# Two SSM convolution layers and two GEGLU layers on one core: another opening, and filter transforms moved from the opening into the layers

## The chip, the cores and the metric

The kernel runs on one core of a Trainium2 chip. The metric is the device time of one execution in microseconds. The engines are TensorE (PE, with its weight loads PEld), VectorE (DVE), ScalarE (ACT), GpSimd (POOL) and SyncE (SP); SP, ACT and POOL also issue DMA transfers, each in the order of its own queue. An instruction runs when its engine has come to it and what it waits for is done; the order on each engine is fixed when the program is built.

## The reference

Two kinds of layer alternate, A, B, A, B, over x of 2048 tokens by 576 channels; B's feed-forward width is 4608. All inputs are bf16.

```python
def _A_ref(q, k, v, shift_k, ssm_k, ssm_D):
    k_shift = sum over t in range(4) of k_pad[:, t:t + S, :] * shift_k[:, 3 - t]
    kv = k_shift * v
    y = causal convolution of kv with ssm_k along the tokens (by rfft2/irfft2 of length 2 * S)
    y = y + kv * ssm_D
    return q * y
def _B_ref(x, w_gate, w_up, w_down):
    return (_gelu(x @ w_gate) * (x @ w_up)) @ w_down

x = A_q
x = x + _A_ref(_layernorm(x), A_k, A_v, A_shift_k, A_ssm_k, A_ssm_D)
x = x + _B_ref(_layernorm(x), B_w_gate, B_w_up, B_w_down)
x = x + _A_ref(_layernorm(x), A_k, A_v, A_shift_k, A_ssm_k, A_ssm_D)
x = x + _B_ref(_layernorm(x), B_w_gate, B_w_up, B_w_down)
```

The convolution's result y does not depend on x: both A layers use the same y, computed once.

## The kernel before

**Convolution.** Tokens are cut into 4 blocks of 512. A block is transformed by matmuls with tables of cosines and sines (512 odd frequencies; kt is a tile of 128 frequencies of four, s is the cosine or the sine part). The spectrum of the product of k-block a and filter block b is added to output block a + b. `kv_ops` (L152 to L179) makes a block of kv on DVE: per pair of token rows four tap products (L162), three adds (L167) and a product with v (L172). `fwd_eo` (L201) transforms a block of kv: for kt 0 and 1 it sums even and odd token rows apart in PSUM, ACT copies them out, and two DVE operations (`cross`, L213) make kt and kt + 2 of them, so that four matmuls serve where eight would. `prod` (L217) multiplies spectra on DVE, `accumulate` (L231) sums products in PSUM by an identity matmul, `both`, `shifted` and `inverse` lead back to y.

**The opening** (`begin`, L475 to L691) is written out by hand. It makes a table G for the filter (angles on DVE, a mask, sines on ACT, four rounds, L534 to L541) and tables F1, F2 for kv. All four filter blocks are transformed in it (`h_tile`, `fwd_h` L181: eight matmuls for each kt and s, 16 tiles of 2 x 8) and stored in DRAM (Hd); block 1 also stays in SBUF (H1). Filter block 0 comes by a plain load and PE transposes (L551), blocks 1 to 3 by transposing DMAs on SP (L494). k block 0 is loaded by ACT's queue after two small loads, v block 0 by POOL's. Then come the kv of block 0, its transform (`fwd_full`, L190, with a negated copy of two token rows, L590), products (L224 to L228), pairs (L625), the inverse, the gate of layer A for the first 512 tokens (L792, L797), their normalising (L1003) and transposes into xnT (L1015). Between these stand the filter tiles of blocks 1 to 3 and the first 8 of the 16 kv operations of block 1.

**The layers.** The work of B is cut into 8 units (layer, block of 512 tokens) and each unit into 3 phases of 12 gate/up groups (18 matmuls of 512 columns, L1096) and the down projection (96 matmuls, L1112). Passes are [0], [1, 2], [3, 4], [5, 6], [7]: in a pass the phases are the outer loop, so pass 0 is unit 0 alone, and unit 1, tokens 512 to 1023 of the first B layer, is the first that needs y of block 1. Its xnT is written by transposing DMAs on SP (`spread`, L924).

**The planner.** `Pace` keeps an estimated clock for PE, DVE and ACT while the program is built. `fill` (L979) is called after each gate/up group and within the down projection. It issues due weight loads, loads of the convolution in the order of the list L (`run_loads`), tasks of DVE from two lists (`conv.run_v`: V with U ahead; `run_vq`: gates and normalising) as long as they end before a limit, and up to three pieces of PE work of the convolution (`run_p`, list Pq, in order). `conv.step(m)` enters block m in these lists. One PSUM buffer ("cps") is the convolution's, three ("pr") are the layers'. `load_k` and `load_v` have one SBUF buffer each (tags "k" and "v" of the pool c_kv).

## Time and profile before

| | |
|---|---|
| median of 3 runs | 964.27 us (962.89 to 965.34) |
| profiled execution, span | 963.7 us |
| first gate/up matmul (L1096) | 68.15 us |
| first gate/up matmul of unit 1 | 192.74 us |
| gate/up, L1096 | 5184 matmuls, 566.2 us |
| down, L1112 | 2304 matmuls, 296.9 us |
| filter transforms, L186 | 256 matmuls, 27.6 + 10.1 us, all before 68.3 us |
| transforms of kv in the layers, L207 | 96 matmuls, 15.7 us |
| sums of products, L234 | 144 matmuls, 24.7 us |
| PE busy, 0 to 10 / 10 to 20 / 20 to 30 / 50 to 60 us | 10.0 / 8.79 / 8.31 / 6.84 |
| DVE busy, 30 to 40 / 50 to 60 / 70 to 80 / 100 to 110 us | 9.69 / 4.62 / 7.82 / 8.97 |

Busy time of a line is the union of its instructions' spans. The spans of neighbouring matmuls overlap in the trace (two sums of L234 have 0.42 us together), so what a matmul costs in a stream is read from the period, one start to the next. A name like cps<-v,F is the output and the inputs by the program's names.

### The profile page before, as it was taken

Reading aid. Unit: us, or ns where it says so; the run is one execution under the profiler, and the core shown is the slowest. Engines: PE = TensorE matmul, PEld = TensorE weight load, DVE = VectorE, ACT = ScalarE, POOL = GpSimd, SP = SyncE. Lnnn points to the kernel's source line nnn. Section 1 sums busy time; section 2 is a strip of 40 time slices with the busy share of each in tenths; the row PEclk is TensorE's granted clock in tenths of the full one; section 3 lists DMA queues with packets and bytes.
Section 4 is the critical chain, followed back from the end, with each engine's and each line's share of the span. In section 5 each row is a group of like instructions: output and inputs, shape, how many; then the busy total and the mean of one; then the engine's idle time right before and its main releaser. Section 6 shows DMA issues by size and latency. Waiting matters only on the chain.

```text
span 963.7 us, 19315 instructions
## 1 busy us (share of the span) xinstructions
PE 948.0 (98%) x8256; PEld 546.6 (57%) x8256; DVE 538.8 (56%) x975; ACT 304.5 (32%) x557; POOL 139.7 (14%) x303
## 2 busy tenths in 40 slices
PE   6989999999999999999999999999999999999998
PEld 4764655646556566465565565565466466456455
DVE  7967887988785476888323333654323325522332
ACT  7866223541222523413212412342211213311211
POOL 2453210432101111412000100230000002100000
PEclk9999999999999999999999999999999999999999
DMA  6979994693942641495270270484450540396630
GB/s 166 312 192 287 300 199 126 112 224 134 264 148 75 130 131 49 100 240 129 51 170 3 57 166 7 90 147 105 89 134 1 100 123 2 77 253 148 155 71 26
DMA packets 129066, 127.48 MB, mean 132 GB/s; under 512 B 45587, under 2 KB 121684, under 8 KB 128980
## 3 DMA queue, kind: packets, MB, share of 16 engines
q1 hardware_dynamic: 119904, 90.85, 43.5%
q0 software_dynamic: 8944, 34.49, 11.0%
q8 instruction: 64, 1.05, 0.5%
q10 hardware_dynamic: 132, 0.91, 0.3%
q14 instruction: 22, 0.18, 0.1%
HBM read 105.58 MB, written 10.62 MB: 121 GB/s over the span
## 4 chain that ended last, share of the span: by engine, by line
PE 95%; DVE 3%; DMA 1%; ACT 1%; POOL 0%; issue 0%; SPq 0%; DVEq 0%
PE gu L1096 58%; PE dn L1112 30%; PE cps L234 2%; PE cps L207 1%; PE cps L260 1%; PE ps L186 1%; DMA hn<-in_A_ssm_k_dram 1%; PE cps L186 0%; DVE yb L228 0%; DVE prod L227 0%; DVE yb L625 0%; DVE stats L777 0%; DVE kvt L162 0%; DVE prod L224 0%; PE xps L1015 0%
## 5 line engine op out<-in xcount | busy, mean ns | idle before, releaser
L1096 PE MATMUL gu<-xnT,wgu 64*128 64x512 bf16 x5184 | 566.2, 376 | 0.0
L1096 PEld LDWEIGHTS <-wgu 64*128 64x128 bf16 x5184 | 249.1, 94 | 307.1 <-issue 9.0
L1101 DVE TENSOR_TENSOR hT<-ga,gu 128x512 bf16<-128x512 f32 x288 | 197.7, 687 | 265.2 <-ACT ga L1100 263.7
L1100 ACT ACTIVATE ga<-gu 128x512 f32<-128x512 f32 x288 | 172.0, 597 | 540.9 <-PE gu L1096 539.0
L1112 PE MATMUL dn<-wd,hT 128*128 128x288 bf16 x2304 | 296.9, 286 | 0.5 <-DVE ob L1121 0.5
L1112 PEld LDWEIGHTS <-hT 128*128 128x128 bf16 x2304 | 223.6, 98 | 66.2 <-issue 10.5
L1146 DVE TENSOR_TENSOR x_c<-x_c,dn 128x576 f32<-128x576 f32 x64 | 48.2, 753 | 92.5 <-PE dn L1112 92.1
L825 POOL TENSOR_SCALAR nm<-s 128x1 f32<-128x1 f32 x60 | 19.9, 332 | 369.9 <-DVE x_c L1141 170.6
L833 ACT ACTIVATE junk<-x_c,nm 128x576 bf16<-128x576 f32 x48 | 36.9, 769 | 27.4 <-POOL nm L825 27.4
L841 POOL TENSOR_TENSOR rstd<-ve,neghalf_t 128x1 f32<-128x1 f32 x60 | 38.3, 638 | 5.0
L228 DVE TENSOR_TENSOR sum<-prod 128x576 bf16<-128x576 bf16 x72 | 33.0, 458 | 3.1
L186 PEld LDWEIGHTS <-G 128*128 128x128 bf16 x256 | 26.1, 103 | 10.2 <-DVE h L553 1.3
L186 PE MATMUL ps<-h,G 128*128 128x288 bf16 x192 | 27.6, 300 | 1.8 <-DVE h L553 1.2
L318 POOL DMA_DIRECT2D kr<-Kd x24 | 13.2, 548 | 107.4 <-DVE prod L227 107.4
L1132 DVE TENSOR_TENSOR ob<-x_c,dn 128x576 bf16<-128x576 f32 x15 | 11.3, 755 | 29.0 <-PE dn L1112 19.9
L326 POOL DMA_DIRECT2D hr<-Hd x32 | 17.7, 553 | 52.8 <-DVE prod L227 52.7
L840 POOL TENSOR_SCALAR ve<-ss 128x1 f32<-128x1 f32 x60 | 17.7, 294 | 51.2 <-ACT junk L833 51.1
L234 PE MATMUL cps<-sum,ident 128*128 128x288 bf16 x144 | 24.7, 286 | 0.0
L162 DVE TENSOR_TENSOR kvt<-k,skc 128x1152 bf16<-128x1152 bf16 x32 | 23.8, 754 | 0.5
L215 DVE TENSOR_TENSOR kc<-eo 128x288 bf16<-128x288 f32 x48 | 19.4, 453 | 2.5 <-ACT eo L210 2.5
L210 ACT COPY eo<-cps 128x576 f32<-128x576 f32 x24 | 15.3, 637 | 16.4 <-PE cps L207 13.6
L268 POOL DMA_DIRECT2D out_dram<-ob x12 | 6.7, 555 | 88.0 <-DVE ob L1132 88.0
(114 smaller groups left out, 471.9 us busy)
## 6 DMA issues: line engine op xcount, KB each, us to landing
wgu<-in_B_w_gate_dram SPq DMA_DIRECT2D x45, 576.0 KB, 5.6
wd<-in_B_w_down_dram SPq DMA_DIRECT2D x30, 864.0 KB, 7.2
wgu<-in_B_w_up_dram SPq DMA_DIRECT2D x45, 512.0 KB, 7.5
hr<-Hd POOLq DMA_DIRECT2D x32, 288.0 KB, 6.6
kr<-Kd POOLq DMA_DIRECT2D x24, 288.0 KB, 5.2
Hd<-h POOLq DMA_DIRECT2D x12, 288.0 KB, 3.8
Kd<-kc POOLq DMA_DIRECT2D x12, 288.0 KB, 8.9
k<-in_A_k_dram POOLq DMA_DIRECT2D x3, 1008.0 KB, 10.4
```

Of the source, the lines that this page charges most:

```text
L162: nc.vector.tensor_tensor(out=st[dst][:], in0=self.kt_[b][:, s0:s0 + 2, :], in1=self.skc[:, j, :].unsqueeze(1).to_broadcast([P, 2, D]), op ...
L186: nc.tensor.matmul(ps[:, h, 0:HW], lhsT=G[:, i, s * NFQ + kt * P: s * NFQ + (kt + 1) * P], rhs=src[:, i, h * HW:(h + 1) * HW], start=(i == ...
L228: nc.vector.tensor_tensor(out=dst, in0=pr[:, 0, :], in1=pr[:, 1, :], op=ALU.subtract if part == 0 else ALU.add)
L234: nc.tensor.matmul(ps[:, h, 0:HW], lhsT=self.ident[:], rhs=pr[:, h * HW:(h + 1) * HW], start=first, stop=last)
L825: nc.gpsimd.tensor_scalar(out=v["nm"][:], in0=v["s"][:], scalar1=-1.0 / D, scalar2=None, op0=ALU.mult)
L833: nc.scalar.activation(out=junk[:], in_=get_x(), func=ACT.Square, bias=v["nm"][:, 0:1], accum_out=v["ss"][:])
L841: nc.gpsimd.tensor_tensor(out=v["rstd"][:], in0=ve[:], in1=neghalf_t[:, 0:1], op=ALU.pow)
L1096: nc.tensor.matmul(pair[:, s, :], lhsT=w[r0:r0 + HK, k, gi * P:(gi + 1) * P], rhs=xnT[r0:r0 + HK, b, :], start=(k == 0), stop=(k == NKC - 1))
L1100: nc.scalar.activation(out=ga[:], in_=pair[:, 0, :], func=ACT.Gelu_apprx_tanh)
L1101: nc.vector.tensor_tensor(out=hT[:, fi, :], in0=ga[:], in1=pair[:, 1, :], op=ALU.mult)
L1112: nc.tensor.matmul(acc[:, h, 0:HW], lhsT=hT[:, fi, j * P:(j + 1) * P], rhs=wd[2 * wb + fi // WT][:, fi % WT, h * HW:(h + 1) * HW], start=( ...
L1146: nc.vector.tensor_tensor(out=xh, in0=xh, in1=acc[:, :, 0:HW], op=ALU.add)
```

## The change

The function `begin` is gone. The opening is now written as tasks with an engine, a cost, dependences, PSUM banks and a priority; a class `Plan` puts them in order by a list schedule when the program is built, and then they are issued in that order. What the tasks do differs too:

- One table T of 128 frequencies (`tang`, `tmask`, `tsin`) and one table V for the way back serve everything. The other three tiles of frequencies are T with the planes exchanged or negated (`turned`, `fw`, `lhs`); DVE makes the negated planes (`tnegs`, `vnegs`). The filter is read in the token order of kv, so G, F1 and F2 fall away.
- The taps of k block 0 are multiplied on DVE, and the four products of a token row are summed in PSUM by identity matmuls; v multiplies that sum from PSUM.
- The skip weight ssm_D is added to the filter before its transposes, on POOL, from a load of single columns (`dcol`).
- Only filter block 0 is transformed in the opening, and sent to DRAM. Block 1 is loaded and transposed there by PE (`turned_h(1)`) into the buffer of tag "v". Blocks 2 and 3 are read by a transposing DMA on SP and written to DRAM again in natural order (`natural`, hs). `conv.step(m)` then transforms filter block m by `fwd_h`, which uses `fwd_eo`, so that 4 matmuls serve where 8 did, as 8 pieces in Pq ahead of the pieces of kv; Hd is stored after it, and hr is loaded from Hd for every pair (block 1 is no longer resident). v of block m is loaded after those pieces, into the same buffer.
- All 16 kv operations of block 1 are in the layers.
- The inverse of block 0 stays in PSUM and the gate reads it there; ACT copies y out afterwards.
- The first three gate/up groups are cut in two: their halves for token rows 0 and 2 (256 columns) stand in the opening, the halves for rows 1 and 3 in the layers' loop. These three and the convolution's bank take the four PSUM banks.
- The queues: k block 0 is the first load on ACT's; sk1, the small parts of k, the filter, v, x_b and filter block 1 go by SP's, followed by wgu 0, wgu 1, filter block 2, wgu 2 (after block 1's transposes), wd 0, wd 1, filter block 3, wd 2.

The core of the diff:

```diff
+    def order(self, cold):
...
+            task.rank = task.cost + task.lat + max([u.rank for u in task.users_of], default=0.0)
...
+            for eng, found in seen.items():
+                first = min(at for at, _ in found)
+                at, task = max(((at, k) for at, k in found if at <= first + 0.25), key=lambda f: (f[1].rank + f[1].prio, -f[0]))
...
+    def turned(self, s, r):
+
+        return s ^ (r & 1), r in ((2, 3) if s == 0 else (1, 2))
...
+        def lh():
+            self.load_ht(m, nc.gpsimd)
+            at["h"] = t.pe + 9.0
+        if loaded:
+            at["k"] = at["h"] = 0.0
+        else:
             self.L.append((lambda: self.kv_at.get(m - 1, NEVER), lk))
-            self.L.append((lambda: self.fwd_at.get(m - 1, NEVER), lv))
-        else:
-            at["k"] = at["v"] = 0.0
+            self.L.append((lambda: self.fwd_at.get(m - 1, NEVER), lh))
+        self.L.append((lambda: self.hf_at.get(m, NEVER), lv))
...
+        def fwd_h(kt, s, h):
+            def run():
...
+                eo = self.fwd_eo(self.ht[m], kt, s, h, 1.0 / NFQ)
...
+                if (kt, s, h) == (1, 1, 1):
+                    self.hf_at[m] = t.pe + 0.49
...
+                    self.cross(eo, hh[kt][:, s, cols], hh[kt + 2][:, s, cols])
...
+                            self.spill(self.Hd[m][k], hh[k], when + LAG)
...
+                    self.Pq.append((lambda: max(get("h")(), NEVER if self.neo > 1 else 0.0), 0.49, fwd_h(kt, s, h)))
...
+    def gu_half(pair, fi, n):
+        gu(pair, wgu[fi // FG], fi % FG, lambda a: a.rearrange("p (j q) -> p j q", q=P)[:, n::2, :], xnT_of[0])
...
+    def natural(b):
...
+        nc.sync.dma_start_transpose(out=h, in_=A_ssm_k[:, b * BS:(b + 1) * BS])
+        nc.sync.dma_start(out=conv.hs[b].rearrange("(r p) d -> p r d", p=P), in_=h)
...
+            K_AT, V_AT, HN_AT = 6.0, 10.0, 8.0
...
+                    mults.append(add("DVE", 0.79, mult, [taps[j]] + mults[-1:] + sum(users[-3:-2], []), ready=K_AT, prio=20.0))
...
+                                nc.tensor.matmul(ps[:, h, 0:HW], lhsT=ident[:], rhs=held["kp", i0, j][:, i - i0, h * HW:(h + 1) * HW],
+                                                 start=(j == conv.KS - 1), stop=(j == 0))
...
+            t0 = turned_h(0, [dadd], HN_AT, 0.0)
+            H0 = {m: filter_tile(m, t0) for m in KTS}
...
+            t1 = turned_h(1, [loads[1]] + [x for m in KTS for x in K0[m]], 0.0, -40.0)
+            for n in range(3):
+                loads.append(add("SP", 2.0, lambda n=n: load_wgu(n), [[], t0, t1][n]))
+                loads[-1].lat = 6.0
+                if n == 1:
+                    loads.append(add("SP", 6.0, lambda: natural(2)))
...
+            order = plan.order({"DVE": 1.2, "ACT": 3.4, "PE": 2.9, "POOL": 3.0, "SP": 4.0})
+            for task in order:
+                task.run()
...
-        for n in range(3):
+        for n in range(2):
             load_wd(n)
-        conv.step(1, kv=conv.kv1[8:], loaded=True)
+        natural(3)
+        load_wd(2)
+        conv.step(1, loaded=True)
```

## The prediction

> **What bounds it now.** I read the page first, then the chain of waits, then the timeline of the opening and of the first pass.

> ```profile
> PE 948.0 (98%) x8256; PEld 546.6 (57%) x8256; DVE 538.8 (56%) x975; ACT 304.5 (32%) x557; POOL 139.7 (14%) x303
> ...
> PE 95%; DVE 3%; DMA 1%; ACT 1%; POOL 0%; issue 0%; SPq 0%; DVEq 0%
> ```

> PE is busy to the end, and the chain is PE nearly throughout. So a time is won only where PE works less, or where it begins the layers earlier. The chain in order of time (start, length, piece) has two parts:

> ```profile
> 26.95 0.76 DVE v L172
> ...
> 45.70 0.74 DVE x_c L792
> ...
> 68.22 15.65 PE gu L1096 x144
> ...
> 269.43 23.42 PE gu L1096 x216
> ...
> 524.39 11.87 PE dn L1112 x96
> ...
> 958.74 1.64 PE dn L1112 x12
> ```

> Up to 45 us the opening is a DVE chain (taps L162/L167, statistics, products, gate). PE fills with filter transforms (L186) whatever waits, and these push the first layer matmul to 68.2. From there PE is packed: 24 visits (8 units by 3 phases) of 23.42 + 11.87 = 35.29 make 847.0, PE ends at 960.4, so 892.2 - 847.0 = 45.2 is the convolution between them. The last 3.3 are the output. 68.2 + 892.2 + 3.3 = 963.7, the span; the median of the runs is 0.6 above.

> The new sum is: start of the layers + 892.2 + added PE work + new waits + 3.3.

> **PE work moved into the layers.** The timeline of the first pass shows what an inserted piece costs:

> ```profile
> 86.44 0.66 PE L207 MATMUL cps<-v,F 128*128 128x288 bf16 x4
> 89.09 0.66 PE L207 MATMUL cps<-v,F 128*128 128x288 bf16 x4
> ...
> 126.69 0.42 PE L234 MATMUL cps<-sum,ident 128*128 128x288 bf16 x2
> 129.09 0.42 PE L234 MATMUL cps<-sum,ident 128*128 128x288 bf16 x2
> ...
> 182.72 0.65 PE L207 MATMUL cps<-v,F 128*128 128x288 bf16 x4
> ...
> 184.19 0.65 PE L207 MATMUL cps<-v,F 128*128 128x288 bf16 x4
> ```

> A gate/up group alone takes 23.42/12 = 1.95; with a forward piece of 4 matmuls the period is 2.65 (so 0.69), with a pair of sums 2.40 (0.45), and amid the down projection 1.47 - 8 x 0.123 = 0.49. Blocks 1 to 3 give 3 x 8 = 24 pieces: between 24 x 0.49 = 11.8 and 24 x 0.69 = 16.6. Block 1 falls wholly among gate/up groups, later ones half in each: **+14.5**. Three groups do their first half (256 columns) in the opening: 3 x 0.98 = **-2.9** (0 if PE then waits as long). Layers: 892.2 + 14.5 - 2.9 = 903.8.

> The other engines take these up: ACT 24 copies of 0.64, with ACT 32% busy; POOL 18 more DMA issues of 0.55 (12 stores of Hd, 4 loads of hr that block 1 had resident, 2 of the filter), 14% busy; DVE, below. On SP the two transposing loads hold its queue 8.97 each (as at 40.97 us before), each with a store waiting behind it for the landing. Queued behind the first are wgu 2 and the first two wd, issued at about 35 to 39 by that; they are needed at groups 8 and 12, some 18 and 26 after the layers begin. This is hidden with 25 us to spare; without the cover it is about 10 once.

> **The opening.** Rows to cost it (start, duration, engine, line):

> ```profile
> 13.31 3.90 PE L186 MATMUL ps<-h,G 128*128 128x288 bf16 x16 [1.21 <-DVE h L553]
> ...
> 32.50 0.75 DVE L224 TENSOR_TENSOR prod<-kc,h 128x1152 bf16<-128x1152 bf16 x1
> ...
> 45.62 0.82 DVE L792 SCALAR_TENSOR_TENSOR x_c<-x_b,mv,y 128x576 f32<-128x576 bf16 x1
> ...
> 47.28 0.82 DVE L792 SCALAR_TENSOR_TENSOR x_c<-x_b,mv,y 128x576 f32<-128x576 bf16 x1
> ...
> 51.08 0.58 DVE L1003 TENSOR_SCALAR xn<-x_c,nm,rstd 128x576 bf16<-128x576 f32 x1 [0.46 <-POOL rstd L841]
> ...
> 54.71 1.12 PE L1015 MATMUL xps<-ident,xn 128*128 128x128 bf16 x9 [3.16 <-ACT h L188]
> ...
> 58.71 0.67 PE L1015 MATMUL xps<-ident,xn 128*128 128x128 bf16 x9
> ```

> *When k lands.* Before: 11.9, third on ACT's queue and beside v and a transposing load. After it is ACT's first, beside 0.7 MB of k's remainder and the filter: 1.58 MB at the 312 to 239 GB/s of 2 to 6 us is 5.1 to 6.6 from the first packet at 1.8. So 6.9 to 8.4, at worst 11.9: I take 7.5, by the bandwidth. The table's angles, its mask (0.69) and sines (1.15) are over by then; G's four rounds of 1.7 DVE and 1.15 ACT are gone.

> *DVE from there.* Eight tap products 8 x 0.755 = 6.0. The six adds (0.77) and two v products are gone, PE sums instead; four v products read PSUM, nearest L1146 at 0.753: 3.0. So 9.0 where L162 to L172 took 12.1. Negations of planes: 6 small operations between 0.18 (L1005) and 0.58 (L1003), nearer the first, 0.9 with 3.5 as the bad end. Statistics 4.9 (27.63 to 32.50). Products 8 x 1.23 = 9.9. Differences 4 x 0.41 = 1.6. Gates 4 x 1.66 = 6.6 (45.62 to 47.28). Normalising 4 x 0.77 = 3.1, copies of xnT 4 x 0.44 = 1.8. Sum 37.8. Four sums of pairs (1.6) have no one waiting and fit the idle below.

> *Idle.* From the end of a gate's second step to the normalising passed 3.7 (47.36 to 51.08: POOL, ACT, POOL); the last of four can't be covered, less the work left for DVE: 3.0. After it 0.67 transposes and 0.5 copies, half already counted: 0.7. First product after the taps: 2 of PE and 0.65 of ACT, mostly covered by the statistics: 0.5. 7.5 + 37.8 + 3.0 + 0.7 + 0.5 = **49.5**, when the second halves start, against 68.2.

> *PE as the opening's bound.* Filter block 0 and the k forward are 16 x 0.98 = 15.7. Of the filter some 3 to 4 pass while the taps run to 17.4, so the rest ends at about 30; evacuation 0.65 and a last product 1.2 bring 32, DVE itself 33.4. DVE leads by 1.5. The halves come on a PE idle but for a few transposes, and a gap costs more than its length: after 3.16 idle at 54.71 nine transposes took 1.12, not 0.67, and eight matmuls behind them 2.12, not 1.14 (1.4 lost); the sixteen at 13.31 took 3.90, not 1.96 (1.9 lost). I take 1.7 for such a gap. Three halves at half speed end at about 50, beside the last xnT: no term here.

> [...]

> **The first pass: does unit 1 wait?** Unit 1 needs the convolution of block 1. What moved behind the layers' start: eight tap operations, eight forward pieces, their 16 crossings (13 of DVE in all), and v of block 1, which can load only once the filter that holds its buffer is read. Rows of before:

> ```profile
> 142.38 1.42 DVE L242 TENSOR_TENSOR yb<-eo,cps 128x576 bf16<-128x576 f32 x2
> ...
> 152.29 1.56 DVE L247 TENSOR_TENSOR yb<-yb 128x576 bf16<-128x576 bf16 x4
> ...
> 171.60 12.64 SPq L924 DMA_TRANSPOSE xnT<-xn  x8
> ```

> From the layers' start: eight filter pieces, one a group, 18; v lands 9.9 after, 28 to 30; nine tap operations amid the down projection, 38; phase 1 with eight forwards (8 x 2.65 + 4 x 2.40) ends gate/up at 69, down with eight sums at 82.5; phase 2 does five products, two pairs and their shifts at one a group (99 to 103), inverses at 3.13 (gate/up ends 112); first normalised tokens at 116, eight SP transposes 12.6, landed at **130**. PE itself arrives at 112 + 11.9 + 1.0 + up to 3.9 of block 2's filter pieces = 125 to **128.6**, the latter by before's seven pieces at that place. Before: 118 against 124.5. Wait **1.5** (0 to 13).

> **Sum.** 49.5 + 903.8 + 3.3 + 1.5 = 958.1 of span, 958.7 as a median.

> **Rivals.**
> *Late first pass (slower).* The chain above has no slack. Before, the shifts (L247) ran 8.5 after the pairs (143.8 to 152.3), their ready time missed by the planner. Once more that here and unit 1 waits 10, and then 1.7 for the half clock: 958.1 + 8.5 + 1.7 = 968.3, median 968.9. It decides from a slip of some 5. For: each step waits on the last. Against: later phases leave more down projection to catch up.
> *Good opening.* k at 6.0, statistics in gaps before the taps end, filter forward out of DVE's way, tail shorter by 1.5: 44 instead of 49.5, no wait: 951. For: DVE has a gap before k lands. Against: x_b is behind v on SP.
> *The plan misses (it doesn't do what it says).* Orders are fixed by landing times of 6, 10 and 8 written out in the plan; if k lands as before (11.9) or PE blocks on a forward ahead of ready filter work, 4 to 6.5 are lost: 49.5 + 6 gives 964.1, no change.

> **Chances.** Forecast 0.46, good opening 0.20, plan misses 0.14, late first pass 0.20. I count 0.3% (2.9 us) as the least that a measurement tells: under 961.4 faster, over 967.2 slower. Faster: 0.46 x 0.9 + 0.20 = 0.61; same: 0.05 + 0.10 + 0.04 = 0.19; slower: 0.04 + 0.16 = 0.20. The range reaches from the good opening with two more us (949) to the late pass (969); the forecast's own is 954 to 963 (opening 46 to 53).

> **What would show it.** Second halves of the first three groups at 46 to 53 us; DVE unbroken from the taps to the gates; PE without gaps but one before unit 1 of 0 to 3; forward pieces at 0.69 and 0.49. A gap there over 5, or a start after 55, makes the forecast wrong on the slow side; a start before 45 on the fast one.

## The result: 994.91 us, slower by 3.2%

| | before | after |
|---|---|---|
| median | 964.81 us (962.89 to 965.88) | 994.91 us (993.14 to 996.55) |
| ratio, 95% interval | | 1.0322 (1.0298 to 1.0347) |
| profiled execution, span | 963.7 us | 994.8 us |
| start of the layers (after: of the second halves) | 68.2 us | 57.98 us |
| from there to PE's last matmul | 892.2 us | 933.4 us |

The layers do begin 10.2 us earlier. The stretch behind them grew by 41.2. Busy times and the shares of the chain of waits, from the page of after:

```profile
PE 957.0 (96%) x8282; PEld 551.7 (55%) x8282; DVE 547.0 (55%) x1011; ACT 299.6 (30%) x542; POOL 144.1 (14%) x308
...
PE 89%; DVE 3%; DMA 3%; issue 2%; POOL 1%; ACT 1%; SPq 0%; POOLq 0%; DVEq 0%; ACTq 0%
```

PE was 95% of the chain and is 89%; DMA went from 1 to 3%, "issue" from 0 to 2%. So something else than PE now sets the time at some places. Excerpts of the chain (start, length, piece):

```profile
63.10 2.05 PE gu L835 x18
...
192.15 5.37 issue
197.52 25.57 PE gu L835 x216
...
421.12 11.56 DMA Hd<-hh
...
433.76 6.76 DMA out_dram<-ob
441.42 22.53 PE gu L835 x180
...
669.00 2.51 DMA xnT<-xn
671.60 24.96 PE gu L835 x214
...
955.41 23.42 PE gu L835 x216
...
989.77 1.64 PE dn L1302 x12
```

In the layers PE has idle times of over 1 us at three places: 182 to 198, 432 to 441, and 668 to 671. A phase that follows such a place takes longer than the 23.42 of an undisturbed one: 25.57 for the same 216 matmuls at 197.52, 24.96 for 214 at 671.60. That is the halved clock, here around the first place:

```profile
180.00:190.00 10.00, 5.14 (x33) 3.23 (x32) 9.23 (x24) 7.32 (x16) 8.56 (x17) 0.90 0.45 77
190.00:200.00 10.00, 3.60 (x16) 1.29 (x17) 2.06 (x4) 0.68 (x2) 1.53 (x3) 0.50 1.05 255
```

(Busy time by stretch: PE, PEld, DVE, ACT, POOL, then the granted clock, DMA share, GB/s.) PE is busy for 3.60 us between 190 and 200, all of it at clock 0.50.

Two things add up to what each place costs: the time without matmuls, beyond their usual spacing, and what the half clock adds, counted as half of the busy time at that clock (around unit 5, 18 matmuls in 3.41 us at it and 34 in the next 3.41 at the full one; table in the last section). Ahead of unit 1 it is 13.2 + 2.05 = 15.2. (PE's last matmul of the down projection starts at 181.79, unit 1's first at 197.52. In these 15.7 us stand that matmul and five filter pieces, worth 2.6 at full clock; then come 4.1 us at half clock.) At the output stores it is 7.2 + 3.0 = 10.2, ahead of unit 5 3.6 + 1.7 = 5.3; together 30.7. And 933.4 - 30.7 = 902.7, so the layers' work is 1.1 under the forecast (903.8). The misses are the start, 8.5, and the three waits, 15.2 - 1.5 = 13.7, 10.2 and 5.3; less the 1.1 they make 36.6, which is the difference of the spans (994.8 - 958.1 = 36.7).

**Unit 1.** Rows from the timeline (start, length, engine, operation; in brackets the idle time and its releaser):

```profile
171.86 1.14 PE L331 MATMUL cps<-yb,V 128*128 128x288 bf16 x8
...
181.65 12.50 SPq L792 DMA_TRANSPOSE xnT<-xn  x8
```

The last part of y of block 1 leaves PE at 171.9 to 179.5, the transposes of xnT are issued from 181.65 to 194.15, and the first matmul of unit 1 runs at 197.52; PE's last matmul of the down projection had started at 181.79. By the trace the transposes issued up to 187.66 landed 2.5 to 2.6 us after their issue, as far as their landings are recorded. Those issued at 188.93 and 191.87 took 6.2 each, beside two stores of Hd and a load of x_b that POOL issued from 188.92 to 190.14. No run tests whether these transfers made it.

**The output stores.** POOL's queue and PE after:

```profile
419.40 0.62 POOL L232 DMA_DIRECT2D v<-in_A_v_dram  x1 [10.48 <-PE cps L281]
...
422.89 0.54 POOL L339 DMA_DIRECT2D out_dram<-ob  x1 [1.23 <-DVE ob L1322]
...
431.17 0.55 POOL L394 DMA_DIRECT2D kr<-Kd  x1 [5.58 <-DMA v<-in_A_v_dram]
...
433.76 0.55 POOL L339 DMA_DIRECT2D out_dram<-ob  x1 [0.25 <-issue]
434.82 0.55 POOL L339 DMA_DIRECT2D out_dram<-ob  x1 [0.52 <-DMA kr<-Kd]
```

```profile
434.12 2.12 PE L835 MATMUL gu<-xnT,wgu 64*128 64x512 bf16 x18 [1.45 <-DVE ob L1322]
441.42 4.02 PE L835 MATMUL gu<-xnT,wgu 64*128 64x512 bf16 x18 [5.18 <-DVE ob L1322]
```

The first output of the pass is stored at 422.89, the second only at 433.76: between them stand the loads of kr and hr for block 3, and the queue stood 5.58 us at one of them. The tile ob (the output rows) has two buffers, so DVE's third ob waits for the first store to land, and PE waits for DVE to empty a PSUM buffer. Before, the same stores left at 415.57, 419.49, 424.12 and 427.74, without such a hold.

**Unit 5.** The inverses that end y of block 3 run at 626 to 629 and again at 654 to 657 (before: all by 489.5), and the transposes follow at once:

```profile
658.73 11.54 SPq L792 DMA_TRANSPOSE xnT<-xn  x8
670.56 0.39 PE L835 MATMUL gu<-xnT,wgu 64*128 64x512 bf16 x2 [2.54 <-DVE x_c L1331]
```

**The opening.** The rows that answer to the forecast's chain:

```profile
7.41 0.76 DVE L999 TENSOR_TENSOR kvt<-k,skc 128x1152 bf16<-128x1152 bf16 x1
...
35.91 0.65 ACT L1058 ACTIVATE h<-ps 128x576 bf16<-128x576 f32 x1 [1.31 <-PE ps L272]
36.59 0.76 DVE L298 TENSOR_TENSOR prod<-kc,h 128x1152 bf16<-128x1152 bf16 x1 [3.40 <-ACT h L1058]
39.73 1.53 DVE L1144 SCALAR_TENSOR_TENSOR x_c<-x_b,mv,ps 128x576 f32<-128x576 bf16 x2
...
49.74 4.02 PE L835 MATMUL ps<-xnT,wgu 64*128 64x256 bf16 x36 [2.07 <-ACT xnT L1202]
...
53.69 1.14 PE L1196 MATMUL ps<-ident,xn 128*128 128x128 bf16 x9
...
57.98 1.16 PE L835 MATMUL ps<-xnT,wgu 64*128 64x256 bf16 x18 [1.24 <-ACT xnT L1202]
```

k is there at 7.4, as forecast. But DVE stands idle 3.40 us before the last product, waiting for ACT, which waits for PE: PE's list ends last, and the gates begin at 39.73. The terms of the forecast up to there (7.5, 9.0, 0.9, 4.9, 9.9, 1.6 and 0.5) make 34.3, so this is 5.4 late. The other 3.1 us of the 8.5 lie behind the gates.

### The profile page after: what moved, and what is told of

The parts are those of the page before. It is cut to its first block, busy times and chain, and to the rows that moved or that the text cites. A ratio compares the mean times of both kernels' runs of the same rounds, so it can differ in the third digit from the quotient of the medians.

```text
span 994.8 us, 19408 instructions
## 1 busy us (share of the span) xinstructions
PE 957.0 (96%) x8282; PEld 551.7 (55%) x8282; DVE 547.0 (55%) x1011; ACT 299.6 (30%) x542; POOL 144.1 (14%) x308
## 3 DMA queue, kind: packets, MB, share of 16 engines
q8 instruction: 65, 1.06, 0.5%
## 4 chain that ended last, share of the span: by engine, by line
PE 89%; DVE 3%; DMA 3%; issue 2%; POOL 1%; ACT 1%; SPq 0%; POOLq 0%; DVEq 0%; ACTq 0%
PE gu L835 55%; PE dn L1302 25%; PE cps L281 2%; PE cps L308 2%; PE ps L272 2%; DMA Hd<-hh 1%; PE cps L331 1%; PE ps L835 1%; DMA wgu<-in_B_w_up_dram 1%; DMA out_dram<-ob 1%; PE ps L1007 1%; POOL rstd L713 0%; DVE hh L289 0%; DVE g_t L733 0%; DVE x_c L740 0%
## 5 line engine op out<-in xcount | busy, mean ns | idle before, releaser
L835 PEld LDWEIGHTS <-wgu 64*128 64x128 bf16 x5238 | 257.3, 95 | 328.0 <-issue 39.5
L1302 PEld LDWEIGHTS <-hT 128*128 128x128 bf16 x2304 | 223.5, 98 | 66.1 <-issue 10.5
L705 ACT ACTIVATE junk<-x_c,nm 128x576 bf16<-128x576 f32 x44 | 33.8, 768 | 18.4 <-POOL nm L697 18.4
L284 ACT ACTIVATE eo<-cps 128x576 f32<-128x576 f32 x48 | 31.2, 650 | 19.7 <-PE cps L281 14.0
L713 POOL TENSOR_TENSOR rstd<-ve,neghalf_t 128x1 f32<-128x1 f32 x56 | 35.0, 626 | 4.7
L712 POOL TENSOR_SCALAR ve<-ss 128x1 f32<-128x1 f32 x56 | 15.7, 281 | 44.4 <-ACT junk L705 44.4
L281 PEld LDWEIGHTS <-T 128*128 128x128 bf16 x144 | 13.5, 99 | 13.1 <-issue 9.9
L281 PE MATMUL cps<-ht,T 128*128 128x288 bf16 x72 | 15.2, 294 | 5.3 <-ACT eo L284 5.2
L289 DVE TENSOR_TENSOR hh<-eo 128x288 bf16<-128x288 f32 x48 | 19.6, 452 | 1.1 <-ACT eo L284 1.0
L301 DVE TENSOR_TENSOR prod<-kr,hr 128x576 bf16<-128x576 bf16 x48 | 19.7, 452 | 0.0
```

Source lines behind the costliest of these rows:

```text
L281: nc.tensor.matmul(ps[:, e, 0:HW], lhsT=self.fw(kt, s, i), rhs=src[:, i, h * HW:(h + 1) * HW], start=(i == e), stop=(i == e + 2))
L284: nc.scalar.activation(out=eo[:], in_=ps[:, :, 0:HW], func=ACT.Copy, scale=scale)
L289: self.nc.vector.tensor_tensor(out=dst, in0=eo[:, 0, :], in1=eo[:, 1, :], op=op)
L705: nc.scalar.activation(out=junk[:], in_=get_x(), func=ACT.Square, bias=v["nm"][:, 0:1], accum_out=v["ss"][:])
L713: nc.gpsimd.tensor_tensor(out=v["rstd"][:], in0=ve[:], in1=neghalf_t[:, 0:1], op=ALU.pow)
L835: nc.tensor.matmul(cols(pair[:, s, :]), lhsT=w[r0:r0 + HK, k, gi * P:(gi + 1) * P], rhs=cols(xnT[r0:r0 + HK, blk_of[k], :]), start=(k == 0 ...
```

## The experiments

**a_own_buffer: the filter of block 1 gets a buffer of its own, and v of block 1 loads without waiting.** It asks what makes unit 1 late.

```diff
-        self.L.append((lambda: self.hf_at.get(m, NEVER), lv))
+        self.L.append((lambda: self.hf_at.get(m, NEVER) if m > 1 else 0.0, lv))
...
-                            hT[b] = conv.ht[b] = conv.kvp.tile([P, RT, D], BF16, tag="v", name="ht")
+                            hT[b] = conv.ht[b] = xtp.tile([P, RT, D], BF16, tag="xnT", name="ht")
```

> Filter block 1 lies in the free second buffer of xnT, so v of block 1 loads when the layers start and not after the eight filter pieces; the PE work is the same. Theory (the wait of PE before unit 1 comes from the chain filter pieces, v load, tap operations, forward pieces): the tap operations run at once, the convolution of block 1 is some 18 us earlier, the wait of 12.2 us and the half-speed stretch behind it (2.0) go: 995 - 14 = 981. Rival (DVE has too much to do in the first pass, 13 us more than before, whatever the order): the wait shrinks by under 5 us, 990 or more.

Measured: 985.19 us (983.56 to 989.88), ratio 1.0236 (1.0205 to 1.0268). The medians fall by 9.7, which lies between theory and rival; the traces tell more. PE's wait for xnT ahead of unit 1 and its half clock are gone; the inverses of block 1 run at 160.5 to 170.8. From the second halves (58.01) to PE's end (978.32) it is 920.3, 13.1 less than 933.4, of the 15.2 read from the trace; new gaps of 1.78 at 95 and 1.75 at 179 take some. (The traced executions are those of 996.55 and 983.56 us, so 13.1 is more than the medians show.) So the wait ahead of unit 1 is shown to come in the main from the buffer shared by the filter and v, which puts v, and all behind it, after the filter's pieces.

**b_late_hr: the loads of kr and hr may go 9 us behind the last crossing of a block's filter instead of 2.**

```diff
-                            self.hd_at[m] = when + 2.0
+                            self.hd_at[m] = when + 9.0
```

> Loads of a new filter spectrum are entered 9 instead of 2 us after its last crossing, so that POOL's queue does not stand on them ahead of the output stores. Theory (the gaps of PE at 432 to 441 us come from output stores behind those loads on POOL): both gaps (7.2 us) and the half-speed stretch (3.0) go, 995 - 10 = 985; the wait before unit 1 stays. Rival (the gaps come from the output buffers' two slots and slow landings alone): the same 995.

Measured: 988.04 us (986.35 to 989.64), ratio 1.0258 (1.0237 to 1.0279). POOL's queue in this run:

```profile
422.90 0.54 POOL L339 DMA_DIRECT2D out_dram<-ob  x1 [1.23 <-DVE ob L1322]
425.84 0.54 POOL L339 DMA_DIRECT2D out_dram<-ob  x1 [2.40 <-DVE ob L1322]
434.25 0.54 POOL L339 DMA_DIRECT2D out_dram<-ob  x1 [7.87 <-DVE ob L1322]
```

The second store leaves at 425.84 instead of 433.76, the gaps fall from 7.2 to 3.2 (1.70 and 1.72 in the trace, less the usual spacing of matmuls), and no half clock is recorded there (mean clock of the traced execution 0.986, in after 0.982). PE ends at 984.49, 6.9 earlier: 4 + 3.0 of half clock. The medians fall by 6.9 too. So these loads ahead of the stores made that part of the wait. What stays, 3.2, is the third ob waiting for the first store, which takes some 10 us to land here.

**c_no_halves: no halves of the first three groups in the opening.**

```diff
-            for fi in range(3):
+            for fi in range(0):
```

> The first three gate/up groups are not cut: no half stands in the opening. Theory (the halves stand ahead of the last two transposes on PE and run at half clock, so they delay the xnT that the second halves need): the first group starts at 55 instead of the second halves at 58, and the layers have 2.9 more PE work: 995 within 1. Rival (the halves are a gain as meant): start 57 to 58 and 2.9 more, 998.

Measured: 997.25 us (994.79 to 998.71), ratio 1.0348 (1.0321 to 1.0375). The first full group begins at 55.38, 2.6 earlier than the second halves, and the layers then hold the 2.9 that the halves had taken. The two nearly cancel; the medians differ by 2.3 us with intervals that overlap, so a small gain of the halves at most. In the trace the last product comes 0.6 later than in after, and the last xnT 2.6 earlier all the same: the halves hold it back by that much or more.

**d_taps_on_dve: the taps of block 0 added on DVE again, not on PE.** (The identity matmuls go, and per pair of rows three adds and one product with v come back on DVE.)

```diff
-                                nc.tensor.matmul(ps[:, h, 0:HW], lhsT=ident[:], rhs=held["kp", i0, j][:, i - i0, h * HW:(h + 1) * HW],
-                                                 start=(j == conv.KS - 1), stop=(j == 0))
+                        last = add("DVE", 0.77, lambda: nc.vector.tensor_tensor(out=st["acc"][:], in0=st["acc"][:], in1=st["tmp"][:], op=ALU.add),
```

> The taps of k block 0 are summed on DVE as before the change (six additions and two v products of two rows, 6.2 us, for four v products from PSUM, 2.9), and PE does not sum them (32 matmuls less). Theory (PE bounds the opening from 8 to 36 us): the filter transform starts 2 to 3 us sooner, and the layers start at 56 to 58: 993 to 995. Rival (DVE bounds the opening, as forecast): the layers start 3 us later, 998.

Measured: 995.39 us (994.57 to 999.95), ratio 1.0344 (1.0315 to 1.0373). The filter's transform begins at 14.27 instead of 16.60, but at half clock until 18.5; the second halves are at 58.54. The time is neither the theory's nor the rival's, and where the taps are added makes no difference to it that these runs can tell. But the front of the opening moves as PE's list does:

```profile
33.72 0.41 PE L272 MATMUL ps<-h,more 128*128 128x288 bf16 x2
...
34.85 0.76 DVE L298 TENSOR_TENSOR prod<-kc,h 128x1152 bf16<-128x1152 bf16 x1 [0.35 <-ACT h L1049]
```

The last piece of the filter ends on PE at 34.1 instead of 35.9, the last product begins 1.7 earlier, at 34.85, and the gates 1.3 earlier, at 38.46, although DVE has 3 us more to do. It is lost behind: the order built here puts differences (L1088) at 41.39 behind the first gates, so the second pair of gates starts at 47.89 instead of 42.65.

**e_three_waits: the edits of a and b, and the other inverses of block 3 allowed amid gate/up groups once the first has run.**

```diff
-        hurry = lambda: (1, RT - 1) not in conv.y_at
+        hurry = lambda: (1, RT - 1) not in conv.y_at or (3, 0) in conv.y_at
```

> The own buffer for filter block 1, the later loads of new spectra, and, third, the last inverses of block 3 may also stand amid gate/up groups. Theory (each of the three waits in the layers has its own cause and nothing else was lost in the layers): 995 - 13 (unit 1) - 7 (output stores) - 5 (unit 5: gaps 3.6, half clock 1.7) = 970, and PE ends 903.6 + 4 of left gaps after the second halves begin at 58. Rival (the waits share a cause, DVE or DMA overload, and move elsewhere): 978 or more.

Measured: 976.74 us (975.55 to 977.21), ratio 1.0141 (1.0126 to 1.0156). It is between theory and rival. Block 3's inverses now run together, from 611.4 to 621.9, and unit 5's wait is gone; the stores keep 1.48 + 1.72. But ahead of unit 1 some 8.3 us came back (gaps of 0.86, 1.67 and 3.35, less the usual spacing, and half clock from 188.15 to 194.97). Without these waits the layers take 902.2.

**f_warm_pe: 32 and 40 one-row matmuls in PE's idle time of the opening**, to see whether the half clock makes the opening late.

```diff
+                    for _ in range(32 if j == 0 else 0):
+                        nc.tensor.matmul(ps[:, 0, 384:512], lhsT=ones[:], rhs=ones[:], start=True, stop=True)
...
+                    for _ in range(40 if i == 3 else 0):
+                        nc.tensor.matmul(held["y", i][:, 0, 384:512], lhsT=ones[:], rhs=ones[:], start=True, stop=True)
```

> 32 small matmuls of ones behind the taps' broadcast (5 to 8 us) and 40 behind the last inverse (42 to 45 us) keep PE busy; their results are not read. Theory (PE bounds the opening and runs at half clock from 8.3 to 13.9 and from 44.6 to 54.9 for want of work): the filter transform starts 2 to 3 us sooner than 16.6, the second halves at 55 instead of 58: 992. Rival (PE's clock there is hidden by DVE): 995.

Measured: 997.35 us (997.1 to 999.14), ratio 1.0361 (1.0345 to 1.0377). It did not do what it was for: the first batch held the taps' bank and put the sums of kv about 1 us back, and the second ended at 44.73, 2.14 us before the next work, and the clock was half (0.50) again from 47.01 to 57.25. The second batch also stands in the PSUM bank that the gate of the last row reads, and puts that gate back by 0.89. Second halves at 60.48. So it tells nothing of the clock's share. It does bear on what one-row matmuls do to the clock (last section).

**g_halves_behind: the second and third halves wait for the transposes of rows 1 and 3.**

```diff
-                later(lambda me: add("PE", 0.99, me(half_of), early_xn[0] + early_xn[1] + [wg0], bank=True, prio=0.0))
+                later(lambda me: add("PE", 0.99, me(half_of), early_xn[0] + early_xn[1] + [wg0] + txs[2:2 + fi], bank=True, prio=0.0))
```

> The second and third early half stand behind the transposes of the third and fourth token row on PE. Theory (the halves delay the last xnT by holding PE): the last xnT at 55.5 instead of 57.9 and the second halves at 55.7: 992.7. Rival (the halves fill waiting time only): 995.

Measured: 993.44 us (991.78 to 994.33), ratio 1.0311 (1.0292 to 1.0329). Second halves at 57.39 instead of 57.98. The medians differ by 1.5 and the ranges overlap, so the order of the halves is a small part of the 3.1 lost behind the gates.

**h_all: e, f and g together.**

> All of the edits of the three kernels sent with this one. Theory (the causes add up): 995 - 25 - 3 - 2 = 965, no slower than the kernel before the change (963.7) by more than 2. Rival (opening and first pass are limited by DVE): 972 or more.

Measured: 977.94 us (976.83 to 979.21), ratio 1.0156 (1.0139 to 1.0172); second halves at 58.55, and the wait ahead of unit 1 again, longer than in e (gaps 0.87, 2.51 and 5.72). f's cost and g's gain cancel, and the 965 of the theory is 13 away.

**i_three: e, but block 1 keeps its 2 us.**

```diff
-                            self.hd_at[m] = when + 2.0
+                            self.hd_at[m] = when + (2.0 if m == 1 else 9.0)
```

> Three waits taken away, each by its own edit: block 1's h in a buffer of its own, the early loads of a next pass 9 us instead of 2 us behind the last gate for blocks 2 and 3 alone (block 1 keeps the 2 us), and the pieces of block 3's first four products in every phase. Theory (the three waits are separate, and what came back ahead of unit 1 in the run with all blocks' loads delayed was block 1's own loads): second halves at 58, layers 903.6 and some 3 us of rest at the stores, so PE ends at 964 to 967 and the time is 967 to 971. Rival (unit 1's wait came back because VectorE has more to do ahead of unit 1, whatever the loads do): a gap of 5 us or more ahead of unit 1 again, and 974 to 978.

Measured: 974.31 us (972.52 to 974.5), ratio 1.0106 (1.0081 to 1.0132), the best version found; PE ends at 967.4 in the profiled execution (span 970.7), the least of its four runs, so the median is above the range expected. The rival's gap of 5 is not there. But the reason that I gave is not shown either: unit 1's transposes are issued no earlier than in e. First e, then i_three:

```profile
173.94 11.87 SPq L792 DMA_TRANSPOSE xnT<-xn  x8
...
189.31 1.04 PE L835 MATMUL gu<-xnT,wgu 64*128 64x512 bf16 x4 [2.96 <-DMA xnT<-xn]
```

```profile
174.74 11.48 SPq L792 DMA_TRANSPOSE xnT<-xn  x8
...
187.86 8.44 PE L835 MATMUL gu<-xnT,wgu 64*128 64x512 bf16 x76
```

The issue ends at 185.81 and 186.22. The last of the eight lands at 189.27 in e, 4.7 us after its issue, and at 188.09 here, after 3.1; in e a load of x_b was issued beside it, at 185.03, which here follows at 188.57. That this made the 1.2 is not tested. PE comes to unit 1 at about 184.4 in e and at 187.86 here, with one more piece of block 2's filter ahead of it (seven for six) and gaps of 2.15 and 1.75 at 94 and 178. So y of block 1 has no slack in these runs: in e PE is there 3 us sooner and waits for more than 3.

**j_busy: 128-row matmuls in PE's idle time of the opening**, 16 at the start, 26 after the skip weights, 60 behind the last inverse; what f was for.

```diff
+            def busy(task):
+                ps = psum("busy", task)
+                for _ in range(26):
+                    nc.tensor.matmul(ps[:, 0, 0:P], lhsT=ident[:], rhs=ident[:], start=True, stop=True)
...
+                    for _ in range(60 if i == 3 else 0):
+                        nc.tensor.matmul(held["y", i][:, 0, 384:512], lhsT=ident[:], rhs=ident[:], start=True, stop=True)
```

> The changed kernel with 128-row matmuls of the identity added where PE has nothing to do in the opening: 16 at its start, 26 between the taps and the first kv product, 60 behind the last inverse; the one-row matmuls did not hold the granted clock. Theory (the opening is 8 us late in part because PE runs at half clock until 13.9 us and again from 44.6 to 54.9 us): full clock from about 9 us and from 44 to 60 us, second halves at 54 to 56 instead of 58, time 991 to 993. Rival (the opening is set by the chain of gates, statistics and transposes, not by PE's clock): second halves at 57.5 or later, 994 to 996.

Measured: 994.76 us (992.04 to 997.04), ratio 1.0322 (1.0287 to 1.0356). The clock was full at 13.49, hardly earlier than after (13.89), and half again from 47.63 to 57.87: the last filler ends at 45.29 and 3.65 us of idle follow. It stands in the PSUM bank that the gate of the last row reads, and that gate waits for it for 1.91 us. Second halves at 61.24, 3.3 later than after. Unit 1's first matmul is later by 3.0 too (200.49), and these 3 us come back behind it: the output stores cost 8.4 instead of 10.2, the wait ahead of unit 5 0.9 less. The expected full clock did not come about, so this run does not decide.

**k_all: i_three with the edits of j and g.**

> The three edits against the waits, the 128-row matmuls of the opening, and the halves placed behind the transposes. Theory (both parts hold and add): second halves at 54 to 56, no wait but some 3 us at the stores, 963 to 966, so within 0.3% of the kernel before. Rival (the clock sets nothing in the opening): 967 to 971 as the run with the three waits away. Rival (VectorE's load ahead of unit 1): 972 or more.

Measured: 979.54 us (975.92 to 984.0), ratio 1.018 (1.014 to 1.0221); 5.2 over i_three between the medians, with runs 8 us apart. In the traced one PE waited again ahead of unit 1, for the landing of xnT at 189.63, and ran at half clock from 190.34 to 193.75. Its opening is the test that f and j missed: here the clock is full from 9.44, and PE's list starts earlier.

```profile
14.55 2.12 PE L272 MATMUL ps<-h,T 128*128 128x288 bf16 x16
...
35.03 0.76 DVE L298 TENSOR_TENSOR prod<-kc,h 128x1152 bf16<-128x1152 bf16 x1 [2.29 <-ACT h L1064]
```

The filter's transform begins at 14.55 instead of 16.60, 2.05 earlier; the last product follows at 35.03 instead of 36.59, 1.6 earlier, and the second halves at 56.24, 1.7 earlier (some of it by g's order). That is PE as the bound of the opening's first part, as in d, and about what its cold start costs: 2 of the 8.5. (The filler holds back the gate of the last row here too, by 1.91.)

## Why the prediction was wrong

*PE work in the layers, 903.8:* right within 2. 902.7 in after and 902.2 in e without their waits. The prices of a forward piece, 0.49 and 0.69, held. (At those prices block 1 among gate/up groups and the others half in each make 15.0, not 14.5.)

*When k lands, 7.5:* right, 7.4.

*"DVE leads by 1.5", the start at 49.5:* wrong, 57.98. PE led up to the gates. The forecast let PE do "3 to 4" pieces of the filter while the taps ran, and have the rest of its 16 x 0.98 done at about 30, so it counted on a list that starts at 14.3 and holds nothing but the 15.7 of pieces. It had taken the taps' adds from DVE without entering them in PE's list. 28 of the 32 identity matmuls and 20 transposes stand on PE up to 16.5, in part at half clock until 13.89, and the filter begins at 16.60, 2.3 later. From there PE is packed to 35.7: 15.7 of pieces, 24 matmuls of the inverse at 0.122 (2.9) and four late sums (0.5) make 19.1, 3.4 more. So PE's list ends 5.7 late, and the gates begin 5.4 late. That PE's list is what holds them, k_all and d show: each ends the list earlier (k_all by an earlier start, d by taking the sums off PE), and the last product follows by 1.6 and 1.7. The other 3.1 come behind the gates. There the forecast gave the three halves "no term", as done beside the last xnT. They stand ahead of its transposes on PE, and at half clock (0.50 from 44.61 to 54.85): without them (c) the last xnT is there 2.6 earlier. Reordering them (g) recovers 0.6.

Two readings under this step were off. The sixteen matmuls at 13.31 of before do not show what the gap ahead of them cost: the record has the full clock from 16.95 only, and their period is 0.234 us (3.74 for sixteen, up to 17.05), that of the next eight 0.121 (0.97, up to 18.02). And the table of before gives PE as busy for 10.0 us from 0 to 10; it is 4.74.

*"Does unit 1 wait", 1.5 (0 to 13):* the chain without slack stood in the forecast as the rival "late first pass", with 11.7; the size is 15.2. The slip that the rival named was another: the shifts behind the pairs (L321 at 169.6 behind L316 at 164.7) are 4.9 late, not more than before (8.5). Counted from the second halves, PE ended the down projection at 124 and would have been through the pieces behind it at about 127 (forecast 125 to 128.6), but the chain was some 10 us late: inverses at 114 to 121 (forecast 102 to 112), unit 1's first matmul at 139.5 (xnT forecast for 130). Run a shows which link: v behind the filter, which the forecast had in its chain and priced without slack. Taken away, 13.1 come back in the trace, 9.7 in the medians. What makes the wait come back in part in e, h_all and k_all is not shown. The forecast's 1.5 has no term for the clock; the runs have both: in b gaps of 1.70 and 1.72 left it full, in k_all 2.09 us of idle was followed by half clock (last section).

*"Later phases leave more down projection to catch up":* wrong for unit 5. I costed block 1's chain and let blocks 2 and 3 pass at the price of their matmuls. Block 3's chain became longer by its filter, and unit 5 waited 5.3; run e removes it by letting the last inverses run amid gate/up groups.

*"POOL 18 more DMA issues, 14% busy":* the step that hid 10.2. POOL was 14% busy in after too, and its queue still held PE up: the loads of kr and hr of block 3, which now wait for its filter, stand ahead of output stores, the queue stood 5.58 us at one of them, and the second store left at 433.76. Run b takes 6.9 of it away.

*The sum of gain and price:* had nothing waited, the change would give 57.98 + 902.7 + 3.4 = 964.1, no gain. The start won 10.2, and the layers' work grew by 902.7 - 892.2 = 10.5. The gain of the forecast hung wholly on the 8.5 of the opening. i_three agrees: with the three waits mostly gone it is still slower than before by 1.06% (0.81 to 1.32%).

What stays open: why some windows of the opening halved the clock and others as busy did not (below), how much of the halves' 2.6 is their half clock, and what delays the landing of unit 1's last transposes.

## What to carry to other kernels

When work is taken from the engine that you think leads, write it into the list of the engine that gets it, transposes and sums included, before deciding which leads. When a chain is moved into a packed stretch, follow it to every later place where its result or its buffer is awaited, in each pass, and look through the queue that its transfers join for what must not wait: share of busy time said nothing there (POOL 14% busy, 5.58 us at one load). And net the gain against the work moved before hoping for the rest: here 10.2 against 10.5.

## What the runs showed of the hardware

```profile
669.25:672.66 3.41, 1.45 (x12) 0.72 (x14) 0.68 (x2) 0.01 (x1) 1.84 (x6) 1.00 0.35 69
672.66:676.07 3.41, 3.41 (x18) 1.50 (x16) 1.14 (x2) 1.35 (x3) 0.34 (x1) 0.50 0.00 0
676.07:679.48 3.41, 3.41 (x34) 1.82 (x32) 2.37 (x6) 1.72 (x4) 0.83 (x3) 1.00 0.42 84
```

1.45 of 3.41 busy (0.43), and the next 3.41 us are at half clock: 18 matmuls instead of 34. The 3.41 us ahead of the other stretches were 0.14 busy in before, and 0.23, 0.19 and 0.00 in after. Cut into such windows, before and after have 546 at full clock that were followed by full, the least busy 0.60. At half clock, windows 0.00 to 0.75 busy were followed by half again, windows 0.94 and 1.00 busy by full. Counted over the thirteen traces, 39 windows at full clock were followed by half: in 37 of them PE was busy for at most 0.47. Of the 3546 followed by full clock the lowest share was 0.46, the next 0.49. The two left of the 39, 0.71 and 0.81, lie in the opening. Of the 0.81 (h_all) one-row matmuls are 0.70. Of the 0.71 (b_late_hr) 128-column transposes are 0.45; windows of 0.71 in f and i_three, with 0.31 and 0.20 of transposes, were followed by full clock, so for transposes the runs decide nothing.

**In f_warm_pe matmuls of one row kept PE busy, and the clock did not come up.** The record of the clock begins with its first rise; before that the period of the matmuls tells it. From 1.09 to 8.65 PE has one-row matmuls alone, with 0.06 us between them. Behind them eight sums of kv still take 2.08 us (from 9.38), where four take 0.65 at 17.99. In k_all, with 26 128-row matmuls in that place (4.92 to 7.88), a window 0.91 busy ends at 9.44, and from there the clock is full: four sums from 8.17 take 1.14, four from 9.85 take 0.66.

**Idle times under 3.41 us stood ahead of half clock.** In k_all PE was idle for 2.09 us, from 187.59 (its window 0.39 busy), and the clock was half in the next. In before, an idle time of 3.16 stood ahead of it (the window 51.09 to 54.50, 0.46 us busy).

**Two output stores took 10 us to land.** In after, the first of the pass leaves at 422.89 and lands at 433.19 by the trace, 10.3 later; in run b it leaves at 422.90 and lands at 433.08, DVE's third ob waited 7.66 us for it, and the third store leaves at 434.25. Before the change the four stores at this place took 7.1 to 7.8. In after, POOL's queue also stood 5.58 us at a load whose releaser was not its own buffer but the landing of v (430.89), issued eight transfers before it. The issues at 431.99, 432.96 and 434.82 each follow by 0.3 to 0.6 us the landing of the transfer eight places before them (431.70, 432.68 and 434.25). I had taken POOL's issues for 0.55 us each.
